# Another issue order for the start of a clustered attention and softplus FFN

## The chip, the cores and the metric

The kernel runs on one core of one Trainium2 chip. Its time is the device time of one launch in microseconds. Four engines compute: TensorE (PE, matrix products and transposes), VectorE (DVE), ScalarE (ACT) and GpSimd (POOL); SyncE (SP) issues the DMAs. Each engine works through its own queue strictly in order, and an instruction waits, by semaphores, until what it reads is written and what it overwrites has been read.

## The reference, cut to what matters

```python
# attention: 4 batches x 8 heads x 768 positions x 64, 16 clusters per head
q_assign = argmax(q_n . c_n)            # nearest centroid of each query
k_assign = argmax(k_n . c_n)            # nearest centroid of each key
mask     = q_assign[:, :, :, None] == k_assign[:, :, None, :]
scores   = q @ k^T / sqrt(64);  scores = where(mask, scores, -1e9)
attn     = exp(scores - max(scores));  attn = attn / (sum(attn) + 1e-9)
x        = (attn @ v), heads side by side: 3072 tokens x 512
# softplus FFN
h   = x @ w_in                          # 512 -> 2048
g   = max(h, 0) + log1p(exp(-abs(h)))
out = g @ w_out                         # 2048 -> 512
```

Where no key lies in a query's cluster, the query is masked everywhere and attends to all keys alike; the kernel finds such queries by a test for live clusters (below).

## The kernel before, in words

**Numbers.** Each fp32 operand is split into two fp16 halves, a high part (a cast) and a low part (a subtraction of the high part). The products are taken on the halves, so a product in fp32 becomes three in fp16.

**Tiles.** Keys come two heads at a time: "keys 2" are heads 2 and 3 of batch 0, "keys 4" the next two. Queries come four heads and three blocks of 128 at a time. The first queries of all (heads 0 to 3) are worked in two halves of two heads each, `first_q` (L838): half 0 with keys 0, half 1 with keys 2. A score tile is 128 queries of one head against the 768 keys. There are 192, in the order of `t`; the first 36 are "upright": their scores are computed twice, once as queries x keys, for the maximum of each row (matmul m L942, DVE's maximum L954), and once turned, as keys x queries (u L981 and L982), with that maximum brought in by a small transpose (turned L961) and a copy of one row into the queries (the "shift", L967 on ACT or L969 on DVE). ACT takes the exp (ptf L1025), and TensorE multiplies by the values (L1137). The 156 others use one score product (L1051), a maximum (L1067), an exp (L1075) and a DMA transpose of the result. When three of a batch's blocks are done, the first layer (L1212 to L1214), the softplus and the second layer (L1613 to L1615; in part through sums of blocks, L1490 to L1492) of those 384 tokens follow.

**The start.** A pair of key heads is cast, split, transposed on TensorE into PSUM (kT, L508; "kT0" for the halves that the cluster scores use, "kT1" for the other ones), and copied out by ACT or DVE (L480). `nearest` (L542) scores the rows against the centroids (sim, L562 and L563) and finds the nearest: maximum L578, equality L584, a table product L590, maximum L592, equality L594. ACT or DVE marks the keys (L648, L650). `clusters` (L690) then counts on TensorE (L701, L703) which clusters hold keys, and DVE reduces that to `al` (L713). In `first_q`, a query half runs the same steps; then comes the test for live clusters: a minimum with `al` (L868) and a maximum over the clusters (L869), which leaves 1 or 0 for each query, `aq`. POOL multiplies the queries by it (L879 for 64 columns, L886 for one more), TensorE transposes the product (qT1, L899), and a copy (L480) makes it ready for the first scores. So the first m (L942) needs: keys 0 copied, and the first query half through its whole test. From keys 4 on, keys are transposed by DMA (`flip`, L292), which SP issues.

**PSUM.** Most of these matmuls share two rings of two buffers, "s" and "h". A transpose of the first keys or of the queries and a score tile each take the next buffer of "s", and wait until its last reader is done. Which transfer or matmul a buffer comes from is therefore set by the order in which the program asks for it.

**The order.** Nothing schedules at run time. Every piece of work is a Python generator that yields one operation at a time; `Order.run` (L152) holds the operation that each waiting generator would issue next, and `PLAN`, a string with two base-36 digits per operation, says which of them issues now. 3,464 operations are issued in this way; that sets each engine's queue, SP's too, and the order in which buffers are taken. `FILL` says how many fillers `warm` (L254, L257) puts ahead of the n-th operation of TensorE: 128x128 by 120 matmuls of constants into a corner of PSUM that nobody reads. `SWAPPED` names the operations that go to the second of their two engines (`either`, L266). Key names: kT1_2_0 is the copy of the first half of keys 2's second transposes, u0 the shift of tile 0, v2 and w2 subtractions for the low part of values and weights, p36 the same for the exp of tile 36, S1_2 a sum near the end. The loads of one ring of buffers wait, on SP, for the eighth DMA before them.

Of the kernel before, what the change touches and what calls it, by code (L numbers as in the profile page):

```python
# [41 lines left out]
PLAN = (
    "020306c30004050cd30a0000000000000000000101d500d6d40005c4060607070c050100d70001010101d3d3d306d4d4d3d4d8d4d3c5"
    "0101010101dad906060c07d3d3d9d4d3d3d3d306d4d3d4d40a0606060606d4d3d4d40101c305db06dcdcd4d4c4c5d3d30106dec4d307"
    "d30606c51f1fd4d41h1hd41fd4c608081f05080b0b0bc7dd0908c80b1h1j1j1h1f1f1j1l1l1h1h1jc4c3c3c51g1n1l1j1n1i0808081n"
    "090909c31j1l1p1l081n1pc61k071l09c30808c7080cc41r1r0b0b0b0b1n1p1pc908cacb0b1t1r1r0cdfdf1m0b1t0909091n1p1pc51t"
    "1o1rc81t1rc90bdh090909091vdgdjc4c5dhdjdjdj1v1q1q1q1qdkdkdkdldkdi1x1t1t1v1v1q1q1scc1qdmcd1x1z1z1x1vca1x1v1u1z"
    "1xc7c6c61zc61xc8c7c7c6c721211w23231z0a21211z1y210d252023ce0bcfc9cac8cbcc21caca25252723c822c9c9c8ca2723c92325"
    "2927270d2b22220a222925cdce25242b2b29272d29260d0dcccbcccecd2d2729292fcf222b28cc0ace2f2h2f0d2d2f2d2bcb22cccgch"
    "ci2h2j2a0d0d0dcgcg2b2h2dcf0dcf0d0dcd2j2c2d2f2e0dcf0dcf0d0d22cjcd2fcbcb2h2e2e2e2l2j2j0d0d2l2n2nchci2echcgch2g"  # L50
    "2h2h2j2l2n2lcgcgck2jch2nce2p2p2i2l2k2p2l2r2ncicicjci2p2rcdchcl2ncjcj2m2p2t2r0eckckckck2t2p2rcj2e2ecicmcjce2o"
    "2r2r2v2v2t2q2t2v2t2q2q2qcl2x0e0e0e2v2tck2q2q2s2v2v2x2z2z2x2xcmclcmclcm2ucn2q2z312x312w0e0e0e0e0e0e0eco2z2x2z"
    "cl2z330e333131cl2y310fcncn0ecncz33353531cmcmcpcq33czcncococo33dpcn35cz37370f0f0fcoczdqdqdp35303937320e0e0eco"
    "cr0e333537dpcz0hdqdqdq3232323439czcp32cqcpcpcqcq32323539370f0f3b3936dsdsdsczcpcp3739crcq3b0fcrcrcrcr393d0fcz"
    "3bcz3b0ecs3d3d3b0f0f0f3dczdtdt0h3bdudu0f0fdtdt0hcqdt383d0i3d3f3f3aczctcscsducs3f3h3f3f3c3jcz3edv3h3jcscs0gcu"
    "0i0i0i3h3ld03hdwctct3h3hdw3edwcz3j0g3n3e3e3edwczd0ctcu3l3ndv0i3j3l3pdydyct3e3edwd0cu0g0j0kcucu3l3n3ndyczczdz"
    "3gdz0i3p0i0icz3rczcuctcv3l3j3l3p3t3p0g3ndzczdz0i3r3iczdzd03p3pcve0e03t3r3v0ie0cz3ke10jcvcv3tcz3xcve13te23md0"
    "0j3vcvcw3t3re13x3r3t3v3z3zcze1e1e3e3e3e30k0k0k3x3ocze4cw3q3qcz413q3qcwcw0i3ze4e4e4cxcze53qd00n3x0i0i3ve5cwcz"
    "cwe4d0cze7e73x3s3v3x3qe5e6d0410mcye7czczcxcxcxcxcxe60g3u0ke7e7e8d0e9e941410ke9cz0k0k0k0k0k413z3z410k0n0n3q0n"
    "d0cz0mebebeb0m0ld0d0ebebea0gec3w0g0g0gcycy0gcycy0g0g0gd03yd040ea0gcy0g0g0g0ld0420od0424242424242eded0n0n0n0n"  # L60
    "0n0n0n0n0l0l0n0kd0d04343434343eed045cz4545454545eeczef4747474747cz494949494949efd0egczeheh4b4b4b0o0oefd04d4d"
    "4dehehd00l0l0l0l4f4f0l0ld04b4b4d4d4f444h4h4h4hd0eiei4j4j4j464dcz0l0l0l0l4h4l4l4f4fehczejejej48cz4a4hcz0l4n4n"
    "czcz4l4p0p0l4cekekek4p4ecz4e4l4l4j4j4lel4nekekelel4e4e4p4p4pczd0cz4g0p0pem4eemem4e4eem4n4nemczenen4r4r4r4ieg"
# [1628 lines left out]
```

## Time and profile before

| | before |
|---|---|
| time, median of 3 runs | 813.32 us (812.65 to 816.44) |
| profiled execution, its own time | 813.45 us |
| its span | 811.7 us |
| PE busy | 799.6 us (99%), 8086 instructions |
| DVE busy | 599.2 us (74%), 1005 |
| ACT busy | 548.7 us (68%), 851 |
| POOL busy | 471.5 us (58%), 351 |
| DMA | 133.71 MB, mean 165 GB/s |
| granted clock of TensorE | 9 or more tenths in all 40 slices |

The span is the time from the first to the last instruction of the profiled execution; its own time is 1.75 us more. "PE" is matmul work, "PEld" the loading of weights beside it. A row of the timeline tells start and length of a group of equal instructions that follow one another on an engine, and in brackets the idle time of the engine ahead of it with what ended it. Matmul ends are modelled, so the distance between two starts says more than a length.

### The profile page before, as it was taken

The numbers are of one execution on the slowest core, as the hardware profiler recorded it, in microseconds if no ns is written. First come the engines' busy times: TensorE is split into PE (matmuls) and PEld (weight loads), VectorE is DVE, ScalarE is ACT, GpSimd is POOL, SyncE is SP. The second block draws the span as 40 slices with busy tenths as digits, with TensorE's granted clock in tenths as the row PEclk, the third lists the DMA queues.
The fourth block names the chain that finished last, engine by engine and source line by source line (L and its number), as shares of the span: only waits on it lengthen the run. The fifth ranks groups of instructions, "written<-read, shape, count | busy, mean of one in ns | idle before, by whom it ended". The sixth has DMA issues, their size and how long they took to land.

```text
span 811.7 us, 19601 instructions
## 1 busy us (share of the span) xinstructions
PE 799.6 (99%) x8086; PEld 542.6 (67%) x8086; DVE 599.2 (74%) x1005; ACT 548.7 (68%) x851; POOL 471.5 (58%) x351
## 2 busy tenths in 40 slices
PE   8999999999999999999999999999999999999998
PEld 7898976655666666666666656666666656576787
DVE  6889998987976877756675547658555878887795
ACT  6677688865777777648587577677676667645441
POOL 4645455554756577745677685687578552613454
PEclk9999999999999999999999999999999999999999
DMA  9986769999899999999899999999888677830101
GB/s 259 234 184 165 205 151 216 195 227 204 165 190 182 180 202 196 215 204 177 153 177 177 185 185 175 209 203 179 171 159 176 116 143 131 131 60 1 47 1 59
DMA packets 390474, 133.71 MB, mean 165 GB/s; under 512 B 367088, under 2 KB 383984, under 8 KB 390384
## 3 DMA queue, kind: packets, MB, share of 16 engines
q1 hardware_dynamic: 390384, 132.46, 82.6%
q8 instruction: 63, 1.03, 0.5%
q14 instruction: 27, 0.22, 0.1%
HBM read 35.68 MB, written 6.29 MB: 52 GB/s over the span
## 4 chain that ended last, share of the span: by engine, by line
PE 76%; DMA 4%; DVE 3%; ACT 2%; issue 1%; POOL 0%; SPq 0%; DVEq 0%; POOLq 0%; ACTq 0%
PE s L1051 11%; PE h L1212 9%; PE h L1214 9%; PE h L1213 9%; PE o L1613 7%; PE o L1615 7%; PE o L1614 7%; DMA pt<-phl 4%; PE mbank L1141 3%; PE mbank L1143 3%; PE mbank L1142 3%; PE m L1490 2%; PE m L1492 2%; PE m L1491 2%; ACT phl L276 1%
## 5 line engine op out<-in xcount | busy, mean ns | idle before, releaser
L1089 POOL TENSOR_TENSOR phl<-p,phl 128x768 f16<-128x768 f32 x117 | 194.1, 1667 | 124.1 <-ACT phl L276 94.1
L1067 DVE TENSOR_REDUCE negm<-s 128x1 f32<-128x768 f32 x156 | 148.1, 953 | 50.3 <-PE s L1051 48.8
L1075 ACT ACTIVATE p<-s,negm 128x768 f32<-128x768 f32 x156 | 139.4, 896 | 64.4 <-DVE negm L1067 49.1
L1212 PE MATMUL h<-xT,wi 128*128 128x384 f16 x512 | 166.9, 326 | 1.1 <-DVE fg L1249 1.1
L1214 PE MATMUL h<-xT,wi 128*128 128x384 f16 x512 | 167.1, 326 | 0.0
L1213 PE MATMUL h<-xT,wi 128*128 128x384 f16 x512 | 167.0, 326 | 0.0
L276 ACT CAST phl<-p 128x768 f16<-128x768 f32 x145 | 118.7, 828 | 20.3 <-DMA pt<-phl 18.0
L1051 PE MATMUL s<-kt,qt 128*128 128x384 f16 x624 | 126.2, 326 | 0.3 <-ACT p L1075 0.3
L1233 ACT ACTIVATE fa<-h 128x384 f32<-128x384 f32 x128 | 62.2, 487 | 70.9 <-PE h L1214 70.2
L1613 PE MATMUL o<-wo,gh 128*128 128x512 f16 x288 | 109.2, 379 | 0.4 <-DVE ot L1636 0.4
L1615 PE MATMUL o<-wo,gh 128*128 128x512 f16 x288 | 109.2, 379 | 0.0
L1614 PE MATMUL o<-wo,gh 128*128 128x512 f16 x288 | 109.2, 379 | 0.0
L1249 DVE SCALAR_TENSOR_TENSOR fg<-fa,h 128x384 f32<-128x384 f32 x104 | 56.7, 549 | 61.6 <-ACT fa L1234 54.2
L1141 PE MATMUL mbank<-vb,pt 128*128 128x65 f16 x936 | 100.2, 193 | 0.6 <-DMA pt<-phl 0.4
L1142 PE MATMUL mbank<-vb,pt 128*128 128x64 f16 x936 | 100.3, 192 | 0.0
L1143 PE MATMUL mbank<-vb,pt 128*128 128x65 f16 x936 | 100.0, 194 | 0.0
L1141 PEld LDWEIGHTS <-pt 128*128 128x128 f16 x936 | 86.8, 98 | 12.9 <-DMA pt<-phl 2.3
L1142 PEld LDWEIGHTS <-pt 128*128 128x128 f16 x936 | 86.3, 97 | 10.4
L1272 POOL TENSOR_TENSOR gh<-fg,gh 128x768 f16<-128x768 f32 x43 | 71.9, 1673 | 28.1 <-ACT gh L276 28.0
L1143 PEld LDWEIGHTS <-pt 128*128 128x128 f16 x936 | 86.4, 97 | 0.0
L1051 PEld LDWEIGHTS <-qt 128*128 128x128 f16 x624 | 58.4, 98 | 40.3 <-issue 0.6
L1214 PEld LDWEIGHTS <-wi 128*128 128x128 f16 x512 | 50.0, 98 | 33.2
(300 smaller groups left out, 1621.2 us busy)
## 6 DMA issues: line engine op xcount, KB each, us to landing
wo<-in_moe_w_in_dram SPq DMA_DIRECT2D x16, 512.0 KB, 5.0
wo<-in_moe_w_out_dram SPq DMA_DIRECT2D x14, 512.0 KB, 3.5
rawk<-in_k_dram SPq DMA_DIRECT2D x15, 384.0 KB, 4.7
rawq<-in_q_dram SPq DMA_DIRECT2D x15, 384.0 KB, 4.4
rawv<-in_v_dram SPq DMA_DIRECT2D x12, 384.0 KB, 3.9
out_dram<-ot SPq DMA_DIRECT2D x18, 256.0 KB, 2.7
rawv<-in_v_dram SPq DMA_DIRECT2D x8, 192.0 KB, 5.3
pt<-phl SPq DMA_TRANSPOSE x78, 6.0
```

What stands on the lines that cost most here:

```text
L1051: nc.tensor.matmul(st[:, j, :SH], qt[:, s, i], kt[:, s, NT // 2 * j : NT // 2 * (j + 1)], start=(s == 0), stop=(s == 1),)
L1067: yield op("DVE", 950, lambda: nc.vector.tensor_reduce(negm, st[:, :, :SH], AX.XY, ALU.max, negate=True))
L1089: lambda e: e.tensor_tensor(phl[:, u, 1], p32, phl[:, u, 0], ALU.subtract),
L1141: nc.tensor.matmul(av, pt[:, 0, c], vb[:, c, D : 2 * D + 1], start=(c == 0), stop=False)
L1142: nc.tensor.matmul(av[:, :D], pt[:, 0, c], vb[:, c, :D], start=False, stop=False)
L1143: nc.tensor.matmul(av, pt[:, 1, c], vb[:, c, D : 2 * D + 1], start=False, stop=(c == NT - 1))
L1212: nc.tensor.matmul(hp, w[0], x[0], start=(c == 0), stop=False)
L1213: nc.tensor.matmul(hp, w[0], x[1], start=False, stop=False)
L1214: nc.tensor.matmul(hp, w[1], x[0], start=False, stop=(c == NP - 1))
L1613: nc.tensor.matmul(po, g[0], wo[:, f, 0, 0], start=(f == f0), stop=False)
L1614: nc.tensor.matmul(po, g[0], wo[:, f, 0, 1], start=False, stop=False)
L1615: nc.tensor.matmul(po, g[1], wo[:, f, 0, 0], start=False, stop=(f == f0 + NF // 2 - 1))
```

## The change

Nothing is computed otherwise, and the 3,464 operations are the same. Three constants differ: `FILL`, `SWAPPED` and `PLAN`. `PLAN` is new in 17 of its first 18 lines (TensorE's first 110 operations or so have a new order, and behind them stand small moves), in one line of its middle and in five near its end.

```diff
-FILL = {0: 40, 3: 12, 4: 21, 6: 11, 10: 11, 14: 28, 16: 23, 18: 8, 19: 8, 22: 7, 25: 6}
+FILL = {0: 40, 3: 12, 4: 4, 5: 12, 6: 14, 10: 9, 14: 23, 16: 4, 18: 8, 19: 4, 20: 6, 22: 6, 26: 6, 35: 8}
...
 SWAPPED
-  'kT1_2_0', 'u27'
+  'S1_2', 'p36', 'u0', 'u2', 'u12', 'v2', 'w2', 'wh0'
...
 PLAN
-    "020306c30004050cd30a0000000000000000000101d500d6d40005c4060607070c050100d70001010101d3d3d306d4d4d3d4d8d4d3c5"
+    "020306c3070004050cd30a0000000000000000000101d500d6d4000506060100d7000101010101c4d3d3c3060107d4d4010101d3d3d4"
...
```

(`SWAPPED` is given by what leaves and joins the list, the 23 lines of `PLAN` by the first.) `FILL` sums to 175 fillers before and 156 after. The keys that leave or join `SWAPPED` move eleven operations to another engine: kT1_2_0 from DVE to ACT; u0, u2 and u12 from ACT to DVE; u27 from DVE to ACT; wh0 (the cast of a weight block) from ACT to POOL; v2, w2 and p36 from POOL to DVE; S1_2 from DVE to POOL.

The first place is DVE's queue around the test for live clusters of the first query half; sim_k2 is the cluster test of keys 2, q0_0_1 the second query half, aq the test's result. Before:

```order
L868 TENSOR_TENSOR qn1_0_0_127<-qn1_0_0_127,al_0_360 128x6x16
L584 TENSOR_TENSOR qn1_0_0_127<-sim_q0_0_1_375,mx_q0_0_1_399 128x6x16
L578 TENSOR_REDUCE mx_k2_429<-sim_k2_373 128x12
L584 TENSOR_TENSOR sim_k2_373<-sim_k2_373,mx_k2_429 128x192
L590 TENSOR_TENSOR sim_k2_373<-sim_k2_373,tab_78 128x192
L592 TENSOR_REDUCE best_k2_439<-sim_k2_373 128x12
L594 TENSOR_TENSOR sim_k2_373<-sim_k2_373,best_k2_439 128x192
L592 TENSOR_REDUCE best_q0_0_1_434<-qn1_0_0_127 128x6
L869 TENSOR_REDUCE aq_0_0_146<-qn1_0_0_127 128x6
```

And after:

```order
L584 TENSOR_TENSOR qn1_0_0_127<-sim_q0_0_1_369,mx_q0_0_1_391 128x6x16
L868 TENSOR_TENSOR qn1_0_0_127<-qn1_0_0_127,al_0_367 128x6x16
L578 TENSOR_REDUCE mx_k2_425<-sim_k2_400 128x12
L869 TENSOR_REDUCE aq_0_0_147<-qn1_0_0_127 128x6
L584 TENSOR_TENSOR sim_k2_400<-sim_k2_400,mx_k2_425 128x192
L590 TENSOR_TENSOR sim_k2_400<-sim_k2_400,tab_78 128x192
L592 TENSOR_REDUCE best_k2_433<-sim_k2_400 128x12
L594 TENSOR_TENSOR sim_k2_400<-sim_k2_400,best_k2_433 128x192
```

L869 has moved ahead of four steps of keys 2 and one of the second query half; one reduction of keys 2 still stands between it and the minimum, L868.

The second place is TensorE's queue from the last transposes of keys 0 to the first score matmuls (weight loads and repeats left out). Before:

```order
L508 MATMUL kT1_0_1_452<-eye_95,kn1_0_124 128x128
...
L257 MATMUL mbank_117<-ones_102,eye_95 128x120
...
L701 MATMUL sim_k2_373<-kn1_2_138,ones_102 128x192
...
L508 MATMUL kT1_2_0_463<-eye_95,kn1_2_138 128x128
...
L899 MATMUL qT1_0_504<-eye_95,qn2_0_0_128 128x128
...
L508 MATMUL kT1_2_1_512<-eye_95,kn1_2_138 128x128
...
L942 MATMUL m_0_0_545<-kt_0_123,qt_0_0_126 128x384
```

And after:

```order
L508 MATMUL kT1_0_1_443<-eye_95,kn1_0_124 128x128
...
L257 MATMUL mbank_117<-ones_102,eye_95 128x120
...
L899 MATMUL qT1_0_454<-eye_95,qn2_0_0_128 128x128
...
L701 MATMUL sim_k2_400<-kn1_2_138,ones_102 128x192
...
L508 MATMUL kT1_2_0_492<-eye_95,kn1_2_138 128x128
...
L508 MATMUL kT1_2_1_507<-eye_95,kn1_2_138 128x128
...
L942 MATMUL m_0_0_515<-kt_0_123,qt_0_0_126 128x384
```

The transposes of the query half, qT1_0, now stand ahead of the count of keys 2 (L701) and of both transposes of keys 2, and no longer between those two; they take their buffer of the ring "s" from an earlier reader.

The third place is ACT's queue from its copies for keys 2 to the first exps; kn1_4 and kn1_6 are the casts of keys 4 and 6, vb0 and vb1 those of values, wi a weight block. Before:

```order
L480 COPY qt_0_0_126<-qT1_0_504 128x768
L480 COPY kt_2_137<-kT1_2_1_512 128x768
L276 CAST kn1_4_594<-rawk_4_497 128x12x64
L967 ACTIVATE qt_0_0_126<-turned_116 1x128
L276 CAST kn1_6_602<-rawk_6_498 128x12x64
L1025 ACTIVATE ptf_0_0_642<-u_0_0_597 128x768
L1025 ACTIVATE ptf_0_0_642<-u_0_1_644 128x768
```

And after:

```order
L480 COPY qt_0_0_126<-qT1_0_454 128x768
L480 COPY kt_2_137<-kT1_2_0_492 128x768
L480 COPY kt_2_137<-kT1_2_1_507 128x768
L276 CAST vb0_104<-rawv_0_129 128x12x64
L390 ACTIVATE wi_119<-wo_120 128x512
L276 CAST kn1_4_524<-rawk_4_520 128x12x64
L1025 ACTIVATE ptf_0_0_595<-u_0_0_566 128x768
L276 CAST kn1_6_528<-rawk_6_521 128x12x64
```

ACT now copies both halves of keys 2, casts the first values and takes one weight step there; the shift of tile 0 (L967) has left for DVE, and the first exp stands behind the cast of keys 4 alone and ahead of that of keys 6.

## Rows read from the trace of the kernel before

**Rows 1.** Windows: us, then busy time and (instructions) of each engine, PEclk, DMA, GB/s.

```profile
0.00:31.08 31.08, 26.48 (x428) 24.24 (x429) 21.90 (x77) 19.80 (x32) 16.61 (x29) 1.00 0.91 243
31.08:100.00 68.92, 67.02 (x783) 62.24 (x782) 62.48 (x117) 50.61 (x90) 36.16 (x35) 1.00 0.80 191
...
sum 811.70, PE 799.58 PEld 542.62 DVE 599.24 ACT 548.74 POOL 471.49; mean PE 199.89 PEld 135.65 DVE 149.81 ACT 137.18 POOL 117.87
```

**Rows 2.** Timeline of PE: start us, us, engine, line, operation [idle before <-releaser].

```profile
9.16 0.51 PE L899 MATMUL qT<-eye,qn 128*128 128x128 f16 x6
...
9.84 0.74 PE L257 MATMUL mbank<-ones,eye 128*128 128x120 f16 x11
...
18.70 0.49 PE L899 MATMUL qT<-eye,qn 128*128 128x128 f16 x6 [0.45 <-DVE kt L480]
...
20.08 0.50 PE L942 MATMUL m<-kt,qt 128*128 128x384 f16 x2
...
23.53 0.22 PE L981 MATMUL u<-qt,kt 128*128 128x128 f16 x1
...
26.22 1.50 PE L1137 MATMUL mbank<-rawv,ptf 128*128 128x65 f32 x12
...
31.08 0.22 PE L981 MATMUL u<-qt,kt 128*128 128x128 f16 x1
```

**Rows 3.** Timeline of DVE, same columns.

```profile
13.60 0.26 DVE L868 TENSOR_TENSOR qn<-qn,al 128x96 f16<-128x96 f16 x1 [0.41 <-POOL qn L834]
13.94 0.35 DVE L578 TENSOR_REDUCE mx_k<-sim_k 128x12 f32<-128x192 f32 x1
...
15.95 0.24 DVE L869 TENSOR_REDUCE aq<-qn 128x6 f16<-128x96 f16 x1
...
18.00 1.01 DVE L480 COPY kt<-kT 128x768 f16<-128x768 f16 x2
...
22.35 0.55 DVE L480 COPY qt<-qT 128x768 f16<-128x768 f16 x1
...
24.72 0.29 DVE L969 TENSOR_SCALAR qt<-turned 1x128 f16<-1x128 f32 x1
```

**Rows 4.** Timeline of POOL, same columns.

```profile
6.97 1.65 POOL L631 TENSOR_TENSOR kn<-rawk,kn 128x768 f16<-128x768 f32 x1 [3.80 <-ACT kn L276]
...
14.20 0.36 POOL L590 TENSOR_TENSOR qn<-qn,tab 128x96 f16<-128x96 f16 x1 [0.63 <-DVE qn L584]
...
16.86 0.83 POOL L879 TENSOR_TENSOR qn<-qn,aq 128x384 f16<-128x384 f16 x1
17.64 0.23 POOL L886 TENSOR_TENSOR qn<-qn,aq 128x6 f16<-128x6 f16 x1
```

**Rows 5.** Timeline of ACT, same columns.

```profile
15.97 0.34 ACT L648 ACTIVATE kn<-sim_k 128x192 f16<-128x192 f32 x1
...
19.23 0.80 ACT L480 COPY qt<-qT 128x768 f16<-128x768 f16 x1 [1.08 <-PE qT L899]
19.92 0.81 ACT L480 COPY kt<-kT 128x768 f16<-128x768 f16 x1
...
21.87 0.83 ACT L276 CAST kn<-rawk 128x768 f16<-128x768 f32 x1 [1.14 <-DMA rawk<-in_k_dram]
```

**Rows 6.** DMAs of the first 45 and 50 us: issue to landing, us.

```profile
kt<-kn SPq DMA_TRANSPOSE x3, 4.8
...
DMA to landing us min/median/max: 2.4/3.9/6.3
```

**Rows 7.** TensorE's waits, 31.08 to 100 us: us in total, times, longest.

```profile
PE m L942 <- ACT ptf L1025: 0.9, 2, 0.5
```

**Rows 8.** Timeline of DVE, a value and a weight subtraction, same columns.

```profile
122.19 0.95 DVE L467 TENSOR_TENSOR vb<-rawv,vb 128x768 f16<-128x768 f32 x1
...
123.06 0.69 DVE L404 TENSOR_TENSOR wo<-wo 128x512 f16<-128x512 f32 x1
```

**Rows 9.** Chain of waits near 123 us: start us, us, what.

```profile
123.64 4.78 DMA rawk<-in_k_dram
```

More of the change, by code (lines that the diff above doesn't have):

```diff
@@ new lines @@
+SWAPPED = ('E1_0', 'S1_2', 'S1l_1', 'S1l_3', 'S2_1', 'S2_3', 'S2h_0', 'S2l_0', 'S3l_0', 'S3l_2', 'S4_0', 'S4_2', 'S4_3', 'S4h_2', 'S4l_1', 'S4l_2', 'T1a_0', 'T1a_2', 'T1c_0', 'T1c_3', 'T1h_3', 'T1l_1', 'T2a_2', 'T2c_1', 'T3a_0', 'T3a_1', 'T3a_2', 'T3a_3', 'T3b_0', 'T3b_1', 'T3b_2', 'T3c_1', 'T3l_1', 'T3l_3', 'T4c_0', 'T4h_2', 'T4h_3', 'T4l_0', 'T4l_2', 'g0_3', 'g0_5', 'g1_1', 'g2_5', 'g5_7', 'g6_0', 'g6_1', 'g6_4', 'g6_5', 'g6_6', 'g7_1', 'g7_2', 'g7_4', 'g7_5', 'g7_6', 'g7_7', 'gh1_6', 'gh2_4', 'gh3_1', 'gh5_6', 'gh7_0', 'gh7_2', 'gh7_3', 'gh7_5', 'k0_0', 'k0_1', 'k14', 'k18', 'k22', 'kT0_0_0', 'kT0_2_1', 'kT1_2_1', 'm12_2_0', 'm12_3_0', 'm20_4_0', 'm28_7_0', 'm8_2_0', 'm8_3_0', 'p100', 'p101', 'p103', 'p136', 'p170', 'p172', 'p173', 'p175', 'p177', 'p178', 'p180', 'p181', 'p182', 'p183', 'p184', 'p185', 'p186', 'p189', 'p190', 'p191', 'p36', 'p38', 'p39', 'p40', 'p42', 'p45', 'p46', 'p47', 'p59', 'p61', 'p64', 'p67', 'p71', 'p72', 'p79', 'p82', 'p85', 'p89', 'p90', 'p92', 'ph175', 'ph178', 'ph180', 'ph184', 'ph186', 'ph189', 'ph58', 'ph62', 'ph83', 'ph86', 'ph87', 'q0_0_0', 'qT1_1', 'u0', 'u1', 'u11', 'u12', 'u13', 'u2', 'u21', 'u23', 'u31', 'u33', 'u35', 'v2', 'v8', 'vh14', 'vh18', 'w15', 'w19', 'w2', 'w20', 'w23', 'w29', 'wh0', 'wh17', 'wh24', 'wh29', 'wh30', 'wh7', 'wh9', 'x0_2', 'x2_0', 'x6_3', 'x7_0', 'x7_1', 'x7_2', 'x7_3', 'xh0_3', 'xh1_3', 'xh2_3', 'xh3_0', 'xh3_3', 'xh6_3', 'xh7_0', 'zk10', 'zk12', 'zk16', 'zk18', 'zk2', 'zk20', 'zk4', 'zq0_1', 'zq8_2')
@@ L42 @@
 PLAN = (
-    "020306c30004050cd30a0000000000000000000101d500d6d40005c4060607070c050100d70001010101d3d3d306d4d4d3d4d8d4d3c5"
[L44 to L57, printed above, removed]
@@ L58 @@
-    "0j3vcvcw3t3re13x3r3t3v3z3zcze1e1e3e3e3e30k0k0k3x3ocze4cw3q3qcz413q3qcwcw0i3ze4e4e4cxcze53qd00n3x0i0i3ve5cwcz"
+    "020306c3070004050cd30a0000000000000000000101d500d6d4000506060100d7000101010101c4d3d3c3060107d4d4010101d3d3d4"
+    "d8d3d3d3d306d4050cd9d9d4d3d3d3d4c5d40606d306c4d306d30606d40101db06d4d3d3dad4d4070a0c0106c6dc06d306de06dcd4d4"
+    "08d40bc405c5dd081f1h1f1fc71h1f09d41j08081f1f1h1jd41hd40bc80b1jc61h1h1l1l1jc4c40bc5c31g1l1l071n1i1n1j1jc5c5c9"
+    "c309091n1n09091p1pca0808080808081l1lc71k07c6c61n1n1p1r1m1r0b081p1pc3c3dg081p1t0b0b0b1t0b0b0b1r1rc81odfdf1v1v"
@@ new lines @@
+    "1t1q1q1q1qc81tc41r1rcb1x1x09091vc509c9ca1v0bdicc1tdh1t1s0cdh1v1v09090909djdj1u1zdkdkdj1zdjdl1x1xcb1xc9c71x1z"
+    "1z1qcc0c21211wc81z211z21c71y23cccd0ac623210d21c82523dkc6cec9dkc923ca25201qcc2727dmcdc7c7cf0dc82523c922222522"
+    "232929222727250dca252bca2b29292426cecf2d2dca27292d2bcccc272fcb2f2b292d282bcbcb2bcf0d0d0dcgchcb2h2f2f2h2acd0d"
+    "0d0d2d2dcfcf2j2c2e0d0d2h2j2l0d22cf0d0d1qci222e2e2e2l2h2f2f2ncj0d0d0d2h2ncecgchcgchcicgchce2j2j2h2l2n2lcg2ecg"
+    "2g2jck2jch2n2p22052p2i2l2k2p2lcdce2r2ncicicjci2p2rchcl2ncjcj2m2p2t2r0eckckckck2t2p2rcjcdcicm2e2ecjce2o2r2r2v"
@@ new lines @@
+    "2v2t2q2t2v2t2q2q2qcl2x0e0e0e2v2tck2q2q2s2v2v2x2z2z2x2xcmclcmclcm2ucncd2q2z312x312w0e0e0e0e0e0e0eco2z2x2zcl2z"
+    "330e333131cl2y310fcncn0ecncz33353531cmcmcpcq33czcncococo33dpcn35cz37370f0f0fcoczdqdqdp35303239370e0e0ecocr0e"
+    "333537dpcz0hdqdqdq32323234393bczcp32cqcpcpcqcq32323539370f36dsdsds390fczcpcp3739crcq3b0fcr0acrcrcr393d0fcz3b"
+    "cz3b0ecs3d3d3b0f0f0f3dczdtdt0h3bdudu0f0a0fdtdt0hcqdt383d0i3d3f3f3aczctcscscsdu3f3h3f3f3c3jcz3edv3h3jcscs0gcu"
+    "0i0i0i3h3ld0ct3hdwct3h3hdw3edwcz3j0g3n3edv3e3edwczd0ctcu3l3n0i3j3l3pdydyct3e3edwd0cu0gcu0j0kcu3l3n3ndyczczdz"
@@ L59 @@
+    "3gdz0i3p0i0icz3rczctcucv3l3j3l3p3t3p0g3ndzczdz0idz3r3iczd03p3pcve0e03t3r3v0ie0cz3ke10jcvcv3tcz3xe1cv3te23md0"
+    "0j3vcvcw3t3re1cz3r3x3t3v3ze1e1e3e3e3e33z0k0k0k3x3ocze4cw3q3qcz413q3qcwcw0i3ze4e4e4cxcze53qd00n3x0i0i3ve5cwcz"
     "cwe4d0cze7e73x3s3v3x3qe5e6d0410mcye7czczcxcxcxcxcxe60g3u0ke7e7e8d0e9e941410ke9cz0k0k0k0k0k413z3z410k0n0n3q0n"
-    "d0cz0mebebeb0m0ld0d0ebebea0gec3w0g0g0gcycy0gcycy0g0g0gd03yd040ea0gcy0g0g0g0ld0420od0424242424242eded0n0n0n0n"
+    "d0czeb0mebeb0m0ld0d0ebebea0gec3w3y0g0g0gcycy0gcycy0g0g0gd0d0ea0gcy0g0g0g0ld040420od0424242424242eded0n0n0n0n"
@@ L70 @@
     "f30r695wcz63635yczd0f36565650t0t670u0u0s0uf4f4f469cz6b6b6bczf6f66d0w6df667676d5qcz60czf7f76b6d62626262f569f3"
-    "f7696d69cz6f6fcz6h6bczf6f8f8f80r0rf664czfad06f0sfaf9666df5d0f96h0u0s0v0s6h6h6hfa0u0u0ud06j6j0u0u68d0fb0w0w0u"
+    "f7696d69cz6f6fcz6hczf6f8f8f80r0rf664czfad06f0sfaf96b666df5d0f96h0u0s0v0s6h6h6hfa0u0u0ud06j6j0u0u68d0fb0w0w0u"
     "6l6lcz6acz6f6f6hf86j6nf8fcfcfcd0fc6l6l6n6n620ucz6p0z6pd0fdfd0wczfc62626j6j6lfefefe6ccz6e6l0u0s0s0scz6p6e6e6e"
@@ L94 @@
     "aeaeczap1eapaphfhfapapczd0agarararaiaphfhfhfd01e1eatd0hghgcz1eakamavheavczczd0aeard0d0d0ard1d1atd1athihiaoax"
-    "atatatavhhhhhh1ehiavavazhiaqhiaxaxaxaxczczax1ehjb1d0d0azaqaq1eaq1eczazb1b1aqaqazb1aqaz1ehkd1d1d1d1d1czhlb3b3"
-    "b5asd0auawayb5hkhkczhlczhlczczb1b11e1eb5hlhlhmb3b3b7d0hmd11e1e1e1e1ehmb7czb3b5hob5b0b2b7hnhnhnb7b7d1d1b9b9b9"
+    "atatatavhhhhhh1ehiavavazhiaqhiaxaxaxaxczczax1ehjb1d0d0azaqaq1eaq1eczazb11eb1aqaqazb1aqazhkd1d1d1d1d1czhlb3b3"
+    "b5asd0auawayb5hkhkcz1ehlczhlczczb1b11eb5hlhlhmb3b3b7d0hmd11e1e1e1e1ehmb7czb3b5hob5b0b2b7hnhnhnb7b7d1d1b9b9b9"
     "bbbbbbb2b2b2b5czczczbdbfbfhqd0d0b4b6hphpb9b9bbb2b9bdbdbdd0bfd0bhbjhqhpb2bbczczbhbhhrbdd1bdbhbjblhqbfhnb8babl"
     "blbfd1bjhnd1bhbhbjd1bjhshshsd0d0blblbnbnczczhththqhqhthtbpbcd0beczbeczczczbphubnd1bebebebphud1d1b2d1hubnbnhv"
-    "hvbrbrbpbrbgd0bthwblhwd1d1d1d1btbthvbrbiczbkbvbvd0bpbpczczczbebebrbxbxd0d0d1btbtd1hxhyhxbvbzhybmbthxhtczczbo"
-    "hvbxbvhyczczd1d1d1d1hzi0bxbxc1bzhzhzd1bvhvbzi0bqbxbqbzd0i1c1i0bqbqczczc1d0d0d1d1d1i2c1bzd1i2bqc1i2bsd0bqbubw"
+    "hvbrbrbpbrbgd0bthwblhwd1d1btbthvbrbiczbkbvbvd0bpbpczczczd1d1bebebrbxbxd0d0btbthxhyhxbvbzhybmbthxhtczczbod1hv"
+    "bxd1bvhyczczd1d1d1d1hzi0bxbxc1bzhzhzd1bvhvbzi0bqbxbqbzd0i1c1i0bqbqczczc1d0d0d1d1d1i2c1bzd1i2bqc1i2bsd0bqbubw"
     "i0hyczczi3i3d1d1d1d1d1i3i3d0i4d1d1d1c1czczbyd0i5bqi5d1d1d1d1d1d1d1c0c2c2c2c2i5c2czczi6i6hyc2c2d1d1d0d0d0d0i6"
@@ L104 @@
     "ininioioioiod0d0d0d0czczimimioimioiqiqiqird0d0ipipipioikilikczczd0d0czisisisczczczd0iuisiud0itiuczczisiviviv"
-    "ivczd0czili4d0isiviviwiwj0ixiwixixivixizixj2ixiod0d0d0d0d0d0d0d0d0d0d0d0isizisj0iyixivixizj0j4j2j1j3j3j3j1i1"
+    "ivczd0czili4d0isiviviwiwiwj0ixixixivixizixj2ixiod0d0d0d0d0d0d0d0d0d0d0d0isizisj0iyixivixizj0j4j2j1j3j3j3j1i1"
     "j5d0d0d0d0d0irird0d0d0d0d0j7j7d0d0j6j2j1j6j6d0j8j8d0d0d0d0d0d0d0j9jaj9jbj9d0d0d0d0d0jcjdjcjejcd0d0d0d0d0d0d0"
```

1 line of the change is left out of this document (removed).

## The prediction

> **What bounds the kernel now.** I read the busy time by stretch first [rows 1]. TensorE (PE) is the bound: 799.6 of 811.7 us busy, so 12.1 us of idle in all, of which 31.08 - 26.48 = 4.6 lie in the first 31 us, 1.9 in the next 69, and 5.6 in the 712 behind them. No other engine comes near: DVE, the next, is busy 599.2. All that the program can win without removing TensorE work is therefore in those 12.1 us and in the fillers (matmuls that write to an unread corner of PSUM and only keep the array running), all 175 of which stand before 26 us. The second view is the timeline of the start, engine by engine [rows 2 to 5]: there TensorE is not the bound, a chain of small tests on the queries and keys is, and the fillers cover its waits. The fillers' price is that of the row at 9.84: eleven in 0.74, 0.067 us each [rows 2].
>
> The start ends with the first half of the first queries. Its test for live clusters is a minimum (L868) and a maximum (L869) on DVE. Between the two lie 13.60 and 15.95, because the whole cluster test of keys 2 (from 13.94) and one step of the second query half stand between them [rows 3]. POOL then multiplies, 16.86 to 17.87 [rows 4]; TensorE transposes at 18.70, after a wait for DVE's copies of 18.00 [rows 2, 3]; ACT copies, 19.23 to 20.03 [rows 5]; and the first score matmuls start at 20.08 [rows 2], the second pair behind ACT's next copy, 19.92 to 20.73 [rows 5]. From ACT's end at 20.03 to TensorE's start is 0.05, which I use for every hand-over. The profiled execution took 813.45 us against a span of 811.7, and the median of the runs is 813.32, so what I work out on the span is taken off 813.3.
>
> **The change, part by part.** No instruction of work is added or removed. Of the fillers, 19 go (175 to 156), 1.3 us at 0.067, but only where they cover waits, so they count inside the chain below and not beside it.
>
> *The front, a loss.* Keys 2 are now transposed before the first queries. They can't start before POOL has their low part, 6.97 + 1.65 = 8.62 [rows 4]; say 8.66. Before, six transposes of the queries and six of keys 2 start at 9.16 and the fillers behind them at 9.84: 0.68 for twelve, 0.34 for six; 12 fillers are 0.80 [rows 2]. So the queries' transposes start at 9.80 and not 9.16: 0.6 later, and all of the first half's tests with them. (DVE now does a step of the keys 0 test before the queries' low part; that wait is shorter and hidden in this one.)
>
> *The test directly behind its input, the gain.* The minimum comes at 13.60 + 0.6 = 14.20. One reduction of keys 2 (0.35) stays between, so the maximum starts at 14.85 and not 15.95, and ends at 15.1. POOL multiplies from 15.1 to 15.95; its second small multiply, which the transposes need too, now has the table product of the second query half ahead of it, 0.36, so it ends at 15.95 + 0.36 + 0.23 = 16.5 and not 17.87 [rows 4]. The transposes now stand ahead of the keys 2 count and take their PSUM buffer from an earlier copy, so DVE's copies of 18.00 no longer hold them: 16.55 and not 18.70, 2.1 us earlier.
>
> *What is late next.* The score matmuls wait for a PSUM buffer as well, and that one comes from the transposes of the low part of keys 2, now behind. ACT marks keys 2 some 0.8 later than at 15.97 (their test starts later and has the maximum inside it), until 17.1; then it copies the queries, until 17.9. DVE's copy that frees the buffer of keys 2's transposes follows its second query half, until 17.7. So those transposes come at 17.75 and 18.1, ACT copies them in two times 0.8 from 18.3 to 19.1 and 19.9 [rows 5], and the first two score matmuls start at 19.15 and 19.95 instead of 20.08 and some 20.8. Of 2.1 us, 0.9 is left.
>
> *Twelve tiles forward.* Behind them the order itself is shorter: the first tile's maximum is turned right after the second tile's matmuls, and the transposes of the second query half go behind the first tile's second scores. First maximum 19.6 to 20.6, second until 21.5, the shift (now on DVE, 0.29 [rows 3]) until 21.8, second scores at 21.85 and not 23.53 [rows 2]. ACT's exp of them now stands behind the cast of keys 4, which waits for its load: 21.87 + 0.83 = 22.7 [rows 5], so exp until 23.5, the second tile's scores 23.7, and the first product with the values 24.7 instead of 26.22. Then maxima and fillers take some of it back: at 31.08, before, TensorE has done first scores of six tiles, second scores and value products up to tile 2 and 1, and the cluster scores of keys 4. The new order has done just that at 30.1, with 8 new fillers in it (0.5). **Lead 1.0 us.** Keys 4 are no obstacle to it: their transposing DMA is issued once POOL is done, near 24.4, and takes 4.8 [rows 6], so it is there at 29.2, and the new order asks for it at 29.5.
>
> *Behind 31 us.* TensorE's work is the same, and it idles 1.9 us up to 100 us, half of it, 0.9, on ACT's exp [rows 7]. The new order of these tiles is another draw of such waits. From both sides: none of them is left (1.9 gained), or there are twice as many (1.9 lost). I take no difference, the value of the row, and keep both ends.
>
> *Work that changes engine.* DVE gets a value subtraction (0.95), a weight subtraction (0.69), three shifts (0.29 each) and later a score subtraction (0.95 as well), and gives a copy (0.55) and a shift: 2.6 us more, about 1.6 of it before 60 us [rows 3, 8]. It has 31.08 - 21.90 = 9.2 idle before 31 and 6.4 from 31 to 100 [rows 1], which hides it; if that cover were gone, each microsecond would delay a maximum and TensorE behind it, 1.6 at most. At the end one 128x768 sum goes from DVE to POOL, some 0.7 longer, where TensorE is saturated and its reader far behind: nothing. The value subtractions that POOL now does later are not read by the upright tiles before tile 36.
>
> Sum: 813.3 - 1.0 = 812.3.
>
> [...]
>
> **Rivals.**
> - *The lead is given back.* The chain that ended last runs between 112 and 156 us mostly through DVE, ACT and a load of keys, as at 123.64 [rows 9], and not through TensorE; if something there is tied to the loads, the lead meets it and ends. Against it: that load is issued behind a subtraction that follows TensorE's own matmuls, so it would shift too. Time 813.3.
> - *More than the lead.* The waits from 31 to 100 us go as well: 812.3 - 1.9 = 810.4. For: the orders behind them were changed; against: ACT and DVE do the same work there in nearly the same time.
> - *Slower: keys 4 late.* ACT's cast of keys 4 waited 1.14 for its load and held nobody; now the first exp is behind it, the next exp behind that of keys 6. It decides as soon as the load lands later than 21.87. The five loads of keys in the first 50 us took 2.4 to 6.3, median 3.9 [rows 6]; 2.4 above the median would give 812.3 + 2.4 = 814.7. Against it: the same loads stand ahead of it on the queue, in another order.
> [...]
>
> **How the numbers follow.** Forecast 0.55; given back 0.22; more 0.12; keys 4 late 0.08; clock 0.03. The forecast's own range is 812.3 with 0.3 for the hand-overs and 0.9, half of the bound of the waits: 811.1 to 813.5. The range for 8 in 10 takes in the given-back case and, as the unknown waits can be 1.9 either way, goes to 810.2 on one side and, with half of the late keys, to 814.2 on the other. A measurement of this kernel can tell about 0.5% from no change, 4.1 us: 809.2 to 817.4. All five cases lie within; faster needs the lead and more than all waits up to 100 us (0.04), slower two of the late cases at once or one that I have not seen (0.05).
>
> **What would show it.** In the profile after: the first L869 near 14.9, the transposes L899 of the first half near 16.6, the first L942 at 19.2, the first L981 at 21.9, the first value product at 24.7, and the second scores of tile 3, which stood at 31.08, near 30.1; TensorE's idle from there to 100 us near 1.9; and the later rows, such as the first matmuls of the first layer, 1 us earlier. If L942 comes at 20 or later, a step of the start is wrong; if L981 at 31.08 has moved and the end has not, the lead was given back, and the stretch where it vanishes names the cause; an L1025 that waits for a cast of keys is the slower rival; a granted clock under 1.00 the last.

## The result and the profile after

The changed kernel takes 820.22 us (median of 6 runs, 818.34 to 823.06), the kernel before 814.01 us in the same runs: a ratio of 1.0074, 95% interval 1.0049 to 1.0099. It is slower by about 6 us, where I forecast a gain of 1. The profiled execution took 821.10 us with a span of 819.3.

The busy times by stretch, in the columns of [rows 1], show where:

```profile
0.00:31.08 31.08, 27.38 (x409) 24.93 (x410) 22.41 (x78) 20.33 (x33) 12.12 (x26) 1.00 0.89 241
31.08:100.00 68.92, 60.97 (x692) 56.52 (x689) 62.60 (x107) 44.45 (x78) 36.71 (x34) 0.98 0.71 173
100.00:200.00 100.00, 99.22 (x945) 68.57 (x944) 87.23 (x151) 73.80 (x121) 47.66 (x37) 1.00 0.90 200
```

From 31 to 100 us TensorE idles 68.92 - 60.97 = 7.95 us, and not 1.9. DVE is busy as long as before, 62.6 of 68.9 [rows 1], but TensorE gets through fewer matmuls, 692 against 783. The waits of TensorE in that stretch (us in total, times, longest), beside the one row of [rows 7]:

```profile
PE m L942 <- DVE negu L954: 2.3, 3, 1.3
PE turned L961 <- DVE rs L1158: 2.0, 1, 2.0
PE m L942 <- ACT ptf L1025: 1.0, 1, 1.0
PE u L981 <- DVE negu L954: 0.8, 2, 0.4
PE turned L961 <- ACT qt L967: 0.7, 1, 0.7
PE turned L961 <- DVE negu L954: 0.7, 2, 0.5
...
PE turned L961 <- DVE qt L969: 0.3, 1, 0.3
```

Five of these rows name DVE, 6.1 us together. Before, DVE stood for one row:

```profile
PE turned L961 <- DVE rs L1158: 0.5, 1, 0.5
```

So DVE is late with the same sum of busy time: its busy time must hold something else than work. The groups of its two steps for the weights tell what. First the kernel before, then the changed one (by form, 31.08 to 100 us: count, then busy us and mean ns of one, then idle before):

```profile
L396 DVE SCALAR_TENSOR_TENSOR wo<-wo,wi 128x512 int32<-128x512 int32 x13 | 10.1, 794 | 0.1
L392 DVE TENSOR_SCALAR wi<-wi 128x512 int32<-128x512 int32 x13 | 5.7, 472 | 0.1
```

```profile
L396 DVE SCALAR_TENSOR_TENSOR wo<-wo,wi 128x512 int32<-128x512 int32 x13 | 10.7, 839 | 0.1
L392 DVE TENSOR_SCALAR wi<-wi 128x512 int32<-128x512 int32 x13 | 10.0, 789 | 0.0
```

Thirteen equal instructions, L392, cost 5.7 us in one order and 10.0 in the other. One of them alone takes 0.42. The timelines of POOL and DVE of the changed kernel side by side show what the long ones have in common; POOL first:

```profile
52.91 1.55 POOL L404 TENSOR_TENSOR wi<-wo,wi 128x512 f16<-128x512 f32 x1 [2.26 <-ACT wi L276]
...
91.73 1.17 POOL L404 TENSOR_TENSOR wo<-wo 128x512 f16<-128x512 f32 x1
92.85 1.61 POOL L404 TENSOR_TENSOR wi<-wo,wi 128x512 f16<-128x512 f32 x1
```

```profile
53.36 1.38 DVE L392 TENSOR_SCALAR wi<-wi 128x512 int32<-128x512 int32 x1
54.77 0.96 DVE L954 TENSOR_REDUCE negu<-m 128x1 f32<-128x768 f32 x1
...
91.85 1.60 DVE L404 TENSOR_TENSOR wi<-wo,wi 128x512 f16<-128x512 f32 x1
93.37 1.51 DVE L1178 TENSOR_TENSOR xn<-x,xn 128x384 f16<-128x384 f32 x1
94.80 0.95 DVE L954 TENSOR_REDUCE negu<-m 128x1 f32<-128x768 f32 x1
95.67 0.15 DVE L1158 TENSOR_SCALAR rs<-mbank 128x6 f32<-128x6 f32 x1
```

DVE's L392 begins at 53.36, when POOL's subtraction of 52.91 already runs, and ends at 54.74, 0.28 behind POOL's end at 54.46. L404 at 91.85 starts behind POOL's of 91.73 and ends 0.55 behind it; L1178 at 93.37 (0.55 alone) starts behind POOL's of 92.85 and ends 0.42 behind it. So each of these DVE steps ended only behind the POOL step that had begun before it, 0.28 to 0.55 us later, and the profile counts all of its time as busy; that such a step stands still until POOL's has ended is my reading of these rows. It is not so for every DVE step. Over seven profiles (before, changed, e1, e2, e7, e8, e12), the 40 L392 that start beside a running POOL step which ends behind their usual end take 0.76 us more on average, the 184 others 0.02. The maxima, L954, take at most 0.02 more in 34 such starts, and so do the reductions L592 and L915 of `eq_q`, a tile in SBUF, in 59. What sets the two kinds of step apart isn't shown. The price of one meeting, at 53.36, was 1.38 for 0.42.

For each kernel, the DVE steps from 30 to 102 us that take over 0.2 us more than the shortest of their line and shape in the same trace are held for 4.2 us in sum before, and 9.1 after.

By chance the second scores of tile 3 start at 31.08 in both profiles. From there to the second scores of tile 35, at 123.13 before and at 130.50 after, the two kernels do nearly the same work; first before, then after:

```profile
31.08:123.13 92.05, 89.87 (x1003) 80.84 (x1001) 84.14 (x157) 69.19 (x123) 46.58 (x44) 1.00 0.77 186
31.08:130.50 99.42, 91.47 (x1008) 82.43 (x1005) 90.11 (x157) 68.43 (x120) 49.90 (x45) 0.98 0.70 172
```

The stretch is 7.4 us longer, and what lies behind it takes 688.6 us before and 688.8 after. Of the 7.4, 5.8 are TensorE's idle time (7.95 against 2.18) and 1.6 its slower work. DVE does 157 steps in both, and is busy 6.0 us more, as its steps are held 12.3 us instead of 6.4. DVE is not full, though: it still idles 9.3 us there, 7.9 before. What makes TensorE wait is a held step that stands ahead of a result that TensorE needs, as the rows at 53.36, 91.85 and 93.37 show. TensorE computed the next scores at 53.30, but their maximum stood behind L392 until 54.77, and TensorE waited 1.3; at 94 it waited 2.0 for the first step of the division (L1158), behind L404, L1178 and L954. What followed that wait is in the granted clock (columns of [rows 1]):

```profile
92.00:94.00 2.00, 1.88 (x18) 1.65 (x15) 2.00 (x2) 1.84 (x5) 2.00 (x2) 1.00 0.00 0
94.00:96.00 2.00, 0.10 (x1) 0.14 (x2) 1.97 (x4) 0.79 (x2) 1.89 (x2) 0.99 0.73 199
96.00:100.00 4.00, 4.00 (x29) 3.77 (x29) 2.43 (x4) 1.08 (x2) 3.19 (x3) 0.58 0.70 146
```

After the idle stretch TensorE worked at 0.58 of its clock for 4 us, at 0.50 from 96.0 to 99.2. Waits of 1.32 us before 55.79 and of 1.55 before 266.57 in the same profile left the clock at 1.00. Of the six executions, three had a mean clock of 0.998 (820.88, 821.10, 823.06 us) and three of 1.000 (818.34, 818.98, 819.56): 2.1 us between the medians.

### The profile page after: what moved, and what is told of

The parts are those of the page before. It is cut to its first block, busy times and chain, and to the rows that moved or that the text cites. A ratio compares the mean times of both kernels' runs of the same rounds, so it can differ in the third digit from the quotient of the medians.

```text
span 819.3 us, 19557 instructions
## 1 busy us (share of the span) xinstructions
PE 801.8 (98%) x8067; PEld 545.2 (67%) x8067; DVE 610.8 (75%) x1008; ACT 548.4 (67%) x849; POOL 471.6 (58%) x350
## 4 chain that ended last, share of the span: by engine, by line
PE 72%; DVE 4%; DMA 3%; issue 2%; ACT 1%; POOL 1%; SPq 0%; DVEq 0%; ACTq 0%; POOLq 0%
PE s L1051 10%; PE h L1212 8%; PE h L1214 8%; PE h L1213 8%; PE o L1613 7%; PE o L1615 7%; PE o L1614 7%; PE mbank L1141 3%; PE mbank L1143 3%; PE mbank L1142 3%; PE m L1491 2%; PE m L1492 2%; PE m L1490 2%; DMA pt<-phl 2%; POOL phl L1089 1%
## 5 line engine op out<-in xcount | busy, mean ns | idle before, releaser
L1089 POOL TENSOR_TENSOR phl<-p,phl 128x768 f16<-128x768 f32 x116 | 193.6, 1676 | 119.1 <-ACT phl L276 89.8
L1141 PEld LDWEIGHTS <-pt 128*128 128x128 f16 x936 | 86.8, 98 | 12.1 <-DMA pt<-phl 1.5
```

The lines of the kernel that those rows point to most:

```text
L1089: lambda e: e.tensor_tensor(phl[:, u, 1], p32, phl[:, u, 0], ALU.subtract),
L1141: nc.tensor.matmul(av, pt[:, 0, c], vb[:, c, D : 2 * D + 1], start=(c == 0), stop=False)
```

## The experiments

Theory A: from 31 us on the new order lets DVE's steps meet POOL's more often, DVE becomes the bound, and TensorE waits for its maxima. Theory B: the start itself is worse. Theory C: the subtractions v2 and w2, moved to DVE, are the loss. Theory D, from the first results: a wait costs more by the clock that falls after it than by itself. Each ratio is against the kernel before in the same runs.

**e1 and e2: each part of the order alone.** The order was cut at the second scores of tile 3 (31 us).

```diff
 e1: PLAN, FILL, SWAPPED of the changed kernel for its first 178 operations,
     then the rest in the order of before
 e2: those of before for its first 169 operations,
     then the rest in the order of the changed kernel
```

> The changed order up to the second scores of tile 3 (near 31 us), with its fillers; from there on the order, fillers and engines of before (the weight and value subtractions w2 and v2 stay on POOL). Theory A (the loss lies from 31 to 100 us: DVE becomes the bound there, because more of its steps wait for a POOL step that runs beside them, and because v2 and w2 were given to it): 812 to 815.5 us, TensorE's idle time from 31 to 100 us 2 to 3. Theory B (the start itself is worse, its loads land 1 to 2 us later and everything behind pays for it): 818 to 821.

> The order of before up to the second scores of tile 3 (near 31 us), with its fillers; from there on the order and engines of the changed kernel (w2 and v2 on DVE). Theory A: 818 to 821 us, TensorE's idle from 31 to 100 us 6 to 9, and several DVE steps of 0.4 to 0.7 us that take 0.9 to 2.3. Theory B: 812 to 815.

e2 measured 820.14 us, ratio 1.0073 (1.0055 to 1.0092): the whole loss, with the same waits (2.0 for the division, 1.3 for a maximum) and 6.4 us in which DVE's steps are held up to 102 us. The order behind 31 us is enough. But e1 measured 819.30, 1.0086 (1.0065 to 1.0107), where theory A wanted 815.5 at most. Its profile shows another cause, at the joint. TensorE waited 1.16 us for a transposing DMA of queries 4, which had been issued at 33.03 (30.50 before). Windows of e1:

```profile
36.00:38.00 2.00, 0.84 (x10) 0.70 (x10) 1.04 (x2) 0.41 (x1) 2.00 (x3) 1.00 0.77 232
38.00:40.00 2.00, 2.00 (x42) 2.00 (x43) 1.19 (x4) 0.59 (x1) 2.00 (x2) 0.90 1.24 326
40.00:48.00 8.00, 8.00 (x50) 7.45 (x50) 5.12 (x14) 2.41 (x5) 2.59 (x5) 0.50 0.31 84
```

One wait of 1.16, and then a clock of 0.50 for 8 us and of 0.54 for the 2 us behind them. This profile is of e1's slowest execution (824.03 us, mean clock 0.991; the other five have 0.996 to 0.998), and it has two late waits besides, 1.7 us at 265 and 2.2 at 431, with a second fall of the clock behind the latter (by its mean the clock is some 7.4 us short over the span of 822.2, and 38 to 50 us hold 5.1 of that).

**e6 and e7: fillers in those waits.**

```diff
 e6 (on e1):
-FILL = {..., 26: 6, 35: 8}
+FILL = {..., 26: 6, 35: 8, 46: 18}
 e7 (on the changed kernel):
-FILL = {..., 26: 6, 35: 8}
+FILL = {..., 26: 6, 35: 8, 127: 30}
```

> e1 with 18 fillers (1.2 us) ahead of the cluster scores of queries 4, the place where e1's TensorE idled 1.16 us for a transposing DMA and after which its granted clock was 0.5 for some 9 us. Theory D (that clock, and not the wait, is most of e1's loss): no fall there, 813 to 816 us. Theory B (e1's loss comes from its start): 818 to 820.5. If the wait itself counts: 818 to 820.5 as well, with the clock at 1.00.

> The changed kernel with 30 fillers (2.0 us) in TensorE's longest wait, ahead of the turned maximum of tile 26 (near 94 us). Theory A with D: the granted clock stays 1.00 from 94 to 100 us in the profile, the executions that fell (3 of 6, some 2 us longer) vanish, 818 to 819.5 us, still 5 above the kernel before, as the waits for DVE stay. If the clock is the main cause: 813 to 815.

e6: 814.66 us, 1.0032 (1.0009 to 1.0056), and the same window of its profile reads:

```profile
40.00:48.00 8.00, 8.00 (x89) 7.55 (x88) 6.97 (x18) 5.79 (x11) 4.58 (x7) 1.00 0.49 138
```

With eighteen matmuls that compute nothing, the window holds 89 matmuls instead of 50, and the median gives back 4.6 of e1's 6.1 us. That is not the price of the one fall alone: e6's profile has neither of the late waits. Eight of e6's twelve executions have a mean clock of 0.997 or more and take 812.25 to 815.66 us, four have 0.993 to 0.995 and take 819.13 to 821.13. So the new start runs as fast as the old one where the clock holds, and theory B falls; the clock is a main part of e1's loss, how large a one in its other executions isn't shown.

e7: 817.63, 1.0051 (1.0038 to 1.0064), 2.6 us less than the changed kernel, or 1.8 when each is set against the kernel before in its own runs; its clock is 1.00 from 92 to 104 us. Its profile also lacks the changed kernel's wait of 1.55 at 266 us, so that the 2.6 need not be the clock's alone. It came out 0.4 below the range that I gave for A with D, and the clock is not the main cause: 4.4 us stay.

**e8: the joint of e1 mended by order.**

```diff
 e8 (on e1): cluster scores of queries 4 on TensorE
-  after the value product of tile 3
+  after the value product of tile 4
```

> e1 with the cluster scores of queries 4 three TensorE operations later (behind the value product of tile 4), so that their transposing DMA has landed; no fillers added. Theory D and the prediction's first term (the new start leads by 1.0 us at 31 us): 811.5 to 814 us, the granted clock 1.00 from 31 to 60 us. Theory B: 818 to 820.

820.88 us, 1.0091 (1.0057 to 1.0125): the expectation failed. Two executions have a mean clock of 1.000 (816.67 and 816.69 us), four 0.992 to 0.998 (819.66 to 825.73). The profiled one (816.67) was the fastest and keeps its clock at 1.00 through every wait; it shows a wait of 1.3 for a maximum near 43 us, and far behind, where the order is that of before, two more: 1.6 at 258 us and 2.2 at 425. The first, DVE and POOL of e8:

```profile
251.75 1.57 DVE L834 TENSOR_SCALAR n<-eq_q 128x192 f16<-128x192 f16 x1
253.35 1.69 DVE L914 TENSOR_TENSOR eq_q<-eq_q,al 128x192 f16<-128x192 f16 x1
```

```profile
251.36 3.46 POOL L1089 TENSOR_TENSOR phl<-p,phl 128x768 f16<-128x768 f32 x2 [2.99 <-ACT phl L276]
```

The same two steps of the kernel before, ahead of POOL's pair and not behind its start (that pair starts at 254.02 there):

```profile
252.73 0.24 DVE L834 TENSOR_SCALAR n<-eq_q 128x192 f16<-128x192 f16 x1
253.01 0.36 DVE L914 TENSOR_TENSOR eq_q<-eq_q,al 128x192 f16<-128x192 f16 x1
```

0.60 us against 3.26: in e8 the first of the two starts 0.39 behind POOL's pair, before it starts 1.29 ahead of it. A loss by meetings is thus no matter of one place; the changed kernel has both long steps at the same point of its order, e1 and e4 the first of them.

**e4, e5: POOL's hold shortened in both kernels.**

```diff
 e4 (on the changed kernel), e5 (on the kernel before), on POOL only:
-  e.tensor_tensor(part[:, 1], val, part[:, 0], ALU.subtract)
+  e.memset(part[:, 1], 0.0)
-  e.tensor_tensor(vb[:, :, :, :D], vf, vb[:, :, :, D : 2 * D], ALU.subtract)
+  e.memset(vb[:, :, :, :D], 0.0)
```

> The changed kernel, but the low parts of weights and values that POOL computes are set to zero by POOL (a write instead of a subtraction of 1.2 to 1.6 us), so that POOL holds up DVE far less; its output lacks those parts. Theory A: within 2 us of the kernel before with the same edit, 810 to 815 us; the time that DVE's steps take beyond their usual length, 9.0 us up to 102 us in the changed kernel, falls under 4. Theory B, and theory C (v2 and w2 alone, whatever POOL does): 817 to 820.

> The kernel before with the same edit as e4 (low parts of weights and values that POOL computes set to zero). Theory A: 809 to 813.5 us, as TensorE idles only 1.9 us from 31 to 100 us there and little of that is DVE's; theories B and C: the same, so that the difference of about 6 us to e4 stays.

e4: 817.33, 1.0052 (1.0033 to 1.0070); e5: 812.02, 0.9985 (0.9977 to 0.9994). In their profiles theory A holds up to tile 35: DVE's steps are held 1.8 us up to 102 us, TensorE's waits for DVE from 31 to 100 us are 1.7 and not 6.1, and the second scores of tile 35 come at 123.26 in e4 and 122.72 in e5, 0.5 apart, where the changed kernel and the one before stand at 130.50 and 123.13. From tile 3 on, which e4 reached 1.4 us earlier, the stretch is 2.0 us longer than e5's (93.28 against 91.30), where it was 7.4 longer. But the medians are 5.3 apart, and A wanted 2: e4 missed its range, and its time lies in the one that I gave for B and C. Its profile, 815.5 and its fastest execution, has the two late waits of e8 again, 1.7 and 2.2, which come from POOL's L1089, a step that the edit leaves alone; they are 3.9 us together. How the slower executions of e4 lost more isn't shown.

**e10: POOL's hold doubled, on the kernel before.**

```diff
-  e.tensor_tensor(part[:, 1], val, part[:, 0], ALU.subtract)
+  [e.tensor_tensor(part[:, 1], val, part[:, 0], ALU.subtract)
+   for _ in range(2 if e is nc.gpsimd and step < 24 else 1)]
```

> The kernel before, in which POOL does each of the first 24 weight subtractions (1.16 us) twice, so that it is in DVE's way longer; the second one writes the same numbers. Theory A: the time that DVE's steps take beyond their usual length up to 102 us grows from 4.2 to 7 or more, TensorE waits for DVE, 815 to 820 us. If POOL's time is covered, as a busy share of half would have it: 812.5 to 814.

829.09 us, 1.0201 (1.0172 to 1.0231), more than expected. DVE's steps are held 12.1 us up to 102 us; TensorE waits 2.0, 1.5 and 1.4 us for DVE at three places up to 100 us and 2.4 at 134, and its clock is 0.95, 0.93 and 0.88 from 31 to 60, 60 to 100 and 100 to 150. POOL was busy 36.16 of 68.9 us there before [rows 1], and doubling a part of it was not covered at all. The stretch from tile 3 to tile 35 takes 108.77 us, 16.7 more than before, which is the whole loss of the profiled execution; DVE's steps are held 16.8 us there, against 6.4.

**e3, e11, e13: the moved subtractions.**

```diff
 e3 (on the changed kernel):  SWAPPED without 'v2', 'w2'
 e11 (on the kernel before):  SWAPPED with 'v2', 'w2'
 e13 (on e3):                 FILL with 127: 30, as in e7
```

> The changed kernel with the value subtraction v2 and the weight subtraction w2 given back to POOL, everything else as changed. Theory A (collisions of DVE with POOL, to which these two add work): DVE has 1.6 us less to do, POOL 2.8 more that DVE can run into: 817 to 820.5 us. Theory C (the moved subtractions alone): 812.5 to 815.

> The kernel before with the subtractions v2 and w2 on DVE, as the change has them, and nothing else of the change: 1.6 us more work for DVE and 2.8 less for POOL between 30 and 45 us. Theory A (the new order of the steps, not these two, makes DVE late): 812.5 to 815 us. Theory C (their work on DVE is a main part of the loss): 815.5 to 819.

> The changed kernel with both v2 and w2 back on POOL (e3) and the 30 fillers in its longest wait (e7). Do the parts add up? By e7 the fall of the clock is worth 2.6 us, by e11 v2 and w2 1.7: if they add up, 815.5 to 816.5 us, and what is left above the kernel before, some 3 us, belongs to the order of the steps alone. If giving v2 and w2 back is worth nothing (as e3 seemed to show, whose clock fell longer): 817.5 to 818.

e3: 820.56, 1.0099 (1.0078 to 1.0119); e11: 814.88, 1.0019 (1.0009 to 1.0028); e13: 816.93, 1.0042 (1.0027 to 1.0057). On the kernel before the two cost 1.7 us by the medians. Given back, they are worth nothing while the long wait stays (e3's clock was 0.91 from 60 to 100 us in its profile) and 0.7 with fillers in it (e13 against e7; 0.4 when each is set against the kernel before in its own runs, which the intervals don't tell from nothing). e13 ended 0.4 above its range for parts that add up. With the fillers in and the subtractions back, 4.0 us remain over the kernel before in the same runs (812.91), with 3.0 us of waits for DVE from 31 to 100 us. In e13's profile they lie between tile 3 and tile 35: 96.43 us, 4.4 more than before, with DVE's steps held 12.0 us there against 6.4.

**e9: an attempt to mend the order.**

```diff
 e9 (on the changed kernel), DVE's queue:
-  v2, L392, L396, maximum of tile 6     ... w15 (L404), L1178, maximum of tile 26, division
+  maximum of tile 6, v2, L392, L396     ... maximum of tile 26, division, w15 (L404), L1178
   (and L392, L392 behind the maximum of tile 11, L392 behind that of tile 12)
```

> The changed kernel with nine of its DVE steps a few places later in DVE's queue: v2 and the two weight steps behind it go behind the maximum of tile 6, two weight steps (L392) behind the maximum of tile 11, one behind that of tile 12, and the weight subtraction and the subtraction L1178 near 92 us behind the maximum of tile 26 and the division that TensorE waited 2.0 us for. Nothing else moves but what depends on them. Theory A (maxima that queue behind steps held up by POOL): TensorE's waits for DVE from 31 to 100 us fall from 6.1 to under 3 us, the clock stays 1.00, 813.5 to 817 us. Theory B or C: 819 to 821.

821.65 us, 1.0114 (1.0092 to 1.0135). The time in which DVE's steps are held fell from 9.1 to 6.9 us, and nothing was won: a wait of 1.7 for a maximum now stands at 39.9, the clock is 0.88 from 31 to 60 us, and the 2.0 at the division came back as 1.8 for the product behind it (L1166), as the steps pushed back met POOL there.

**e12: is it the lag?**

```diff
-FILL = {..., 25: 6}
+FILL = {..., 25: 6, 36: 14}
```

> The kernel before with 14 more fillers (0.9 us) ahead of the second scores of tile 3, near 31 us, and nothing else: does a mere lag of everything behind 31 us set off the later meetings of DVE and POOL near 250 and 420 us that e4 and e8 showed (some 3 us more)? If it does: 816 to 818 us. If not (the order decides, not the lag): 813.5 to 815.

813.36 us, 1.0003 (0.9994 to 1.0012): nothing. In its profile everything is 1.57 us late at tile 35 (0.9 by the fillers, the rest by its loads), TensorE is 0.84 late at 140 us and 0.07 at 157. A lag of this size alone sets off no later meetings, and this kernel absorbs one of 1.6 us behind 124 us.

## Why the prediction was wrong

*The start: right in its steps.* L869 came 0.44 behind the minimum (15.61 to 16.05), before 2.35; the transposes stood at 17.76, the first L942 at 20.11, the second scores at 22.50, the first value product at 25.61:

```profile
17.76 0.51 PE L899 MATMUL qT<-eye,qn 128*128 128x128 f16 x6 [0.57 <-POOL qn L886]
...
20.11 0.48 PE L942 MATMUL m<-kt,qt 128*128 128x384 f16 x2
...
22.50 0.22 PE L981 MATMUL u<-qt,kt 128*128 128x128 f16 x1
```

Each is 0.6 to 1.2 later than forecast, behind one late transfer: the first queries' loads, issued at 3.12 and 3.58 as before, landed 7.0 us after their issue and not 4.9, and ACT's cast waited for them. That differs between executions (4.9 to 6.6 in the other profiles; with 5.2 in e8 the first second scores come at 21.07). Over all profiles of this start (the changed kernel, e1, e3, e4, e6 to e9, e13) the second scores of tile 3 stand at 29.64 to 31.08, median 30.51, forecast 30.1; with the old start and nothing else changed up to there (the kernel before, e2, e5, e11) at 31.08 to 33.86, median 31.3. The lead is some 0.8 us; I said 1.0. Two errors offset each other in it: the lead at the first second scores is 2.2 by the medians (21.57 against 23.77) and not the 1.7 of my steps, and from there to tile 3 the new start takes 8.57 to 9.36 us and not 8.25. *Keys 4 late* did not decide: ACT's cast of them waited 0.48.

*"Behind 31 us ... I take no difference, and keep both ends": the step that failed.* I bounded the stretch by TensorE's own waits, 1.9 either way, and it lost 7.4 up to tile 35. Those waits say what the old order has left over, not what a new one can make. The term that I put at nothing is the time in which DVE's steps stand behind POOL's. It was visible before the change, 4.2 us of it up to 102 us, and the new order brought it from 6.4 to 12.3 in the stretch; TensorE's idle time there grew by 5.8, and the clock behind the longest of them took 1.6. I had left 0.05 for a slower case that I had not seen.

*"Work that changes engine ... 9.2 idle before 31 and 6.4 from 31 to 100, which hides it": half right.* I priced the lost cover at "1.6 at most", and e11 measured 1.7 for the two subtractions. But idle time in sum hid nothing here: DVE idles 6.3 us from 31 to 100 us after the change as well, and TensorE waits 6.1 us for it all the same. And I read POOL only as the giver of work, never as the engine that holds DVE up; e10 prices that.

*The clock rival: right in kind, wrong in place.* I put it between 17 and 20 us and gave it a chance of 0.03 and 3 us, an estimate of mine. No run shows that term: from 17 to 23 us the clock is 1.00 in the profiles of the kernel before and of the changed one. The fall came at 96 us, behind a wait of 2.0; it took 1.6 us in the profile and 2.1 between the medians of the executions with and without it. The rows at 92 to 100 us show 1.00, an idle stretch, and then 0.58.

*"The lead is given back": a part of the truth.* e12 shows that the kernel absorbs a shift behind 124 us. Whether the lead of 0.8 would have lasted can't be told, since no kernel of these kept it that far without new waits.

So the order behind 31 us is enough for the loss of 6 us (e2), and in the profiles nearly all of it lies between tile 3 and tile 35: 5.8 us of TensorE's idle time, beside 5.9 more in which DVE's steps are held by POOL's, and 1.6 of clock. Shortening POOL's hold takes 7.4 down to 2.0 there (e4 against e5), and doubling a part of it costs 16.7 (e10). The two subtractions cost 1.7 on the kernel before (e11); giving them back to the changed kernel won nothing clear of noise. Open is the end of e4, whose total stayed 5.3 over e5: its profile, of its fastest execution, shows two late waits behind such meetings, 3.9 together. What share of the 4.0 us left in e13 each meeting has stays open too: every order that I tried, e9 too, met POOL in other places.
